# Turning the experts' input rows on VectorE instead of TensorE in a fused attention and mixture-of-experts kernel

## The chip, the cores and the metric

One core of one Trainium2 chip runs the whole kernel. The metric is the device time of one execution in microseconds, lower is better. The engines are named as the profile names them: PE is TensorE (PEld its weight loads), DVE is VectorE, ACT is ScalarE, POOL is GpSimd, and SP only issues DMAs.

## The reference

Packed attention runs first. For each of 8 batches and 8 heads, 32 learned rows p attend to 576 keys and values, and then the 576 queries attend to the 32 packed rows. Its output, 4608 rows x of 512 numbers, goes through a mixture of 8 experts of which each row takes one.

```
p_packed = sm_attn(p, k, v)
out = sm_attn(q, p_packed, p_packed)                    # (8, 8, 576, 64)
x = out.transpose(0, 2, 1, 3).reshape(4608, 512)
logits = x @ w_gate + modality_bias[modality_id]        # 8 experts
e_idx = argmax(logits, axis=1)
gate_w = softmax(logits)[row, e_idx]
for e in range(8):
    mask = e_idx == e
    h = maximum(x[mask] @ w1[e], 0)                     # 512 -> 1024
    out[mask] = gate_w[mask, None] * (h @ w2[e])        # 1024 -> 512
```

All inputs and outputs are float32.

## The kernel before

Attention runs in eight units: four pairs of batches, two groups of four heads each. The order of the instructions of the first six units is written out by hand as a table; behind it a scheduler orders what is left of attention together with the first experts' work. Each unit writes its part of x to a buffer `x_scr` in DRAM (by SP). `routing` (L421 to L478) runs once per pair of batches, when both of its units are through: it finds each row's expert and writes, by nine indirect scatters on POOL (L467), one entry of four words for each row into a list `lst` in DRAM. The list is sorted by expert; an entry holds the number of the row, once for reading x and once for writing the output, and the row's gate weight.

The experts' work goes by slots of 256 rows of one expert, two tiles of 128. Slots 0 and 1 use rows of the first two pairs of batches, slots 2 to 5 of the first three, and the slots from 6 on use all the rest; which expert and which list rows a slot has is read from small tables at run time (`values_load`, L628). With this data 20 slots run; three of them have rows for one tile only (`st_1_half`, L695 to L712).

Slot n passes through these steps:

- `fetch` (L655): POOL loads 256 list entries into a tile `mt` (L657) and then issues two indirect gathers (L659), each of 128 rows of 2 KB from `x_scr` to `xt`, one row to a partition. `run` calls it for slot n + 2 while slot n is under way; there are four `mt` and two `xt`.
- `st_x` (L668): the matmuls want x with its columns on the partitions. PE transposes eight blocks of 128x128 by multiplying with the identity (L672) into `ps_t` in PSUM; ACT copies that, rounded, to the high part of `x_hl` (L674), and DVE writes what the rounding left to the low part (L675).
- `st_1` (L678): h = x w1 as three products (high x high, high x low, low x high) into `ps_h`, 96 matmuls (L685). ACT writes the high part `hh` with the relu (L689), DVE the low part `hl` (L690), once per 128x512.
- `st_2` (L714): the second product, 24 matmuls per tile (L719) into `ps_o`; ACT scales by the gate weight into `ot` (L723), and POOL scatters the 128 rows to the output (L724).

The weights of an expert come by SP, 2 MB each of w1 and w2 (`load_w`, L641), and are split into high and low parts by ACT (L652) and DVE (L653) when the expert changes (`sw`); in this run that is once at the start and three times later.

Engines work through their instructions in order; a wait holds all that is behind it on that engine. PSUM has room for one `ps_t` while attention still runs and for two from slot 6 on.

## Time and profile before

| what | value |
|---|---|
| median of 3 runs | 659.03 us (653.37, 659.03, 663.16) |
| profiled execution, span | 658.5 us |
| last scatter of the output (L724) | starts at 648.54 us, 0.97 us |
| mean granted clock of PE | 0.961 |
| busy: PE, DVE, ACT, POOL | 598.8, 261.5, 238.6, 156.2 us |
| transposes of x, L672 on PE | 168, 279 ns each |
| copies L674 on ACT, differences L675 on DVE | 42 of 588 ns, 42 of 683 ns |
| gathers L659 on POOL | 46, 979 ns each |

The median is of whole executions; the span is that of the one execution whose trace was taken, 0.5 us from it. A transpose's 279 ns is its time from start to end; matmuls overlap, so the steps from one start to the next are shorter. Rows of the profile end with the idle time of the engine ahead of the instruction and with what ended it ("<-ACT hh L689"); "issue" is idle time that no wait in the trace explains, and "remote" a release whose sender the trace does not name.

### The profile page before, as it was taken

How to read it: one execution, taken by the hardware profiler on the slowest of the kernel's cores; microseconds unless marked ns; L12 is line 12 of the kernel's file. 1: busy time of each engine (PE TensorE's matmuls, PEld its weight loads, DVE VectorE, ACT ScalarE, POOL GpSimd, SP SyncE). 2: the span in 40 equal slices, each digit the busy share in tenths (PEclk: the TensorE clock that was granted, in tenths of full speed). 3: DMA queues.
4: the chain of work that ended last, by engine and by line, in shares of the span. 5: the costliest groups of instructions: out<-in, count | busy, mean ns of one | idle time of the engine just before them, and what ended most of it. 6: DMA issues, size and time to landing. Idle time of an engine off the chain costs nothing. (4 is left out here: it accounts for less than half of the span.)

```text
span 658.5 us, 12203 instructions
## 1 busy us (share of the span) xinstructions
PE 598.8 (91%) x4564; PEld 505.9 (77%) x4564; DVE 261.5 (40%) x670; ACT 238.6 (36%) x457; POOL 156.2 (24%) x204
## 2 busy tenths in 40 slices
PE   3899969868689989999999999999999999999983
PEld 3565646535478968889888988998899899889982
DVE  1488958769955422112612016311120121112181
ACT  4677847756612202121612127221121221222271
POOL 3001050256161171211221322221122112122121
PEclk9999988968779998999999999999999999999998
DMA  9989999934843811111590212720110111112011
GB/s 239 277 200 274 314 303 300 292 92 146 317 148 105 295 30 63 49 49 33 198 397 30 66 50 66 290 66 34 50 49 34 50 50 53 45 50 51 35 50 53
DMA packets 74856, 87.11 MB, mean 132 GB/s; under 512 B 26448, under 2 KB 60240, under 8 KB 74768
## 3 DMA queue, kind: packets, MB, share of 16 engines
q1 hardware_dynamic: 64656, 63.79, 32.6%
q0 software_dynamic: 8528, 21.93, 10.6%
q8 instruction: 47, 0.77, 0.5%
q10 hardware_dynamic: 1584, 0.28, 0.2%
q14 instruction: 41, 0.34, 0.2%
HBM read 66.74 MB, written 19.24 MB: 131 GB/s over the span
## 5 line engine op out<-in xcount | busy, mean ns | idle before, releaser
L685 PE MATMUL ps_h<-x_hl,w1h 128*128 128x256 f32 x1088 | 202.1, 287 | 5.7 <-issue 4.9
L685 PEld LDWEIGHTS ps_h<-x_hl,w1h 128*128 128x128 f32 x1088 | 174.4, 195 | 8.5 <-issue 5.9
L685 PE MATMUL ps_h<-x_hl,w1l 128*128 128x256 f32 x544 | 155.8, 286 | 0.9 <-issue 0.8
L690 DVE SCALAR_TENSOR_TENSOR hl<-ps_h,hh 128x512 fp32r<-128x512 f32 x68 | 46.9, 690 | 263.8 <-ACT hh L689 261.4
L719 PE MATMUL ps_o<-w2h,hh 128*128 128x512 f32 x296 | 118.0, 399 | 2.8 <-ACT ot L723 1.6
L719 PE MATMUL ps_o<-w2h,hl 128*128 128x512 f32 x296 | 116.8, 395 | 0.0
L719 PE MATMUL ps_o<-w2l,hh 128*128 128x512 f32 x296 | 115.8, 391 | 0.3 <-DVEq L844 0.3
L685 PEld LDWEIGHTS ps_h<-x_hl,w1l 128*128 128x128 f32 x544 | 106.1, 195 | 1.5 <-issue 1.4
L689 ACT ACTIVATE hh<-ps_h 128x512 fp32r<-128x512 f32 x68 | 40.6, 597 | 179.0 <-PE ps_h L685 148.0
L724 POOL DMA_INDIRECT out_dram<-ot,mt x37 | 40.5, 1096 | 189.0 <-ACT ot L723 120.7
L723 ACT ACTIVATE ot<-ps_o,mt 128x512 f32<-128x512 f32 x37 | 25.4, 687 | 141.3 <-PE ps_o L719 115.1
L659 POOL DMA_INDIRECT xt<-x_scr,mt x46 | 45.0, 979 | 104.0 <-PE ps_t L672 45.2
L719 PEld LDWEIGHTS ps_o<-w2h,hh 128*128 128x128 f32 x296 | 55.7, 188 | 14.2 <-ACT ot L723 2.5
L719 PEld LDWEIGHTS ps_o<-w2h,hl 128*128 128x128 f32 x296 | 55.6, 188 | 11.6
L719 PEld LDWEIGHTS ps_o<-w2l,hh 128*128 128x128 f32 x296 | 55.7, 188 | 10.9 <-DVEq L844 0.6
L233 ACT COPY kT<-ps 128x384 f32<-128x384 f32 x96 | 44.0, 489 | 37.7 <-PE ps L229 20.4
L467 POOL DMA_INDIRECT lst<-meta,dsi x36 | 35.3, 980 | 83.2 <-DVE starts L522 31.4
L675 DVE TENSOR_TENSOR x_hl<-ps_t,x_hl 128x512 fp32r<-128x512 f32 x42 | 27.5, 683 | 19.7 <-ACTq L844 14.8
L229 PE MATMUL ps<-ident,rek 128*128 128x128 f32 x144 | 25.7, 306 | 10.3 <-POOL meta L114 7.0
L354 PE MATMUL ps<-bd,a2T 64*128 64x136 f32 (+1 forms) x320 | 28.7, 313 | 5.0 <-DVE lt L366 4.7
L657 POOL DMA_DIRECT2D mt<-lst x23 | 17.3, 752 | 61.9 <-DMA out_dram<-ot,mt 48.2
L229 PEld LDWEIGHTS ps<-ident,rek 128*128 128x128 f32 x144 | 17.9, 154 | 17.0 <-POOL meta L114 7.0
(189 smaller groups left out, 706.4 us busy)
## 6 DMA issues: line engine op xcount, KB each, us to landing
raw<-in_moe_w_dram SPq DMA_DIRECT2D x24, 1024.0 KB
raw<-in_k_dram SPq DMA_DIRECT2D x16, 512.0 KB
raw<-in_q_dram SPq DMA_DIRECT2D x16, 512.0 KB
ld_v<-in_v_dram SPq DMA_DIRECT2D x16, 512.0 KB
x_scr<-xs SPq DMA_DIRECT2D x16, 512.0 KB
rek<-in_k_dram SPq DMA_DIRECT2D x16, 64.0 KB
req<-in_q_dram SPq DMA_DIRECT2D x16, 64.0 KB
ld_v<-in_v_dram SPq DMA_DIRECT2D x16, 64.0 KB
```

The source lines that it names most:

```text
L229: nc.tensor.transpose(out=t[:, c * P:c * P + P], in_=D_[nm + "r"][:, c0 + c, 2 * pr:2 * pr + 2, :], identity=ident)
L233: nc.scalar.copy(out=T_[:, pr, c0 * P:c0 * P + 3 * P], in_=t[:, :3 * P])
L354: nc.tensor.matmul(xp[rows, pr, z * XW:z * XW + XW], a2T[rs, t0:t0 + n], D_["bd", u][rs, :], start=True, stop=True)
L467: ins = ins_of(nc.gpsimd.indirect_dma_start(out=lst, out_offset=bass.IndirectOffsetOnAxis(ap=dsi[:, c:c + 1], axis=0), in_=meta[:, i * NC ...
L659: ins.append(nc.gpsimd.indirect_dma_start(out=xt[:, t], out_offset=None, in_=x_scr[0:NA[ph] * 2 * S] if ph < 2 else x_scr, in_offset=bass. ...
L675: iv = tt(out=M["xl"][:, :, ts], in0=ps, in1=M["xh"][:, :, ts].bitcast(F32), op=ALU.subtract)
L685: nc.tensor.matmul(ps[:, f], M[a][:, j, (f0 + f) * P:(f0 + f) * P + P], M[b][:, j], start=(n == 0), stop=(n == 3 * KD - 1))
L689: ia = nc.scalar.activation(out=M["hh"][:, fs], in_=ps, func=AF.Relu)
L690: iv = nc.vector.scalar_tensor_tensor(out=M["hl"][:, fs], in0=ps, scalar=0.0, in1=M["hh"][:, fs].bitcast(F32), op0=ALU.max, op1=ALU.subtract)
L719: nc.tensor.matmul(op, M[a][:, j, t * P:t * P + P], M[b][:, j, :], start=(n == 0), stop=(n == 3 * KF - 1))
L723: nc.scalar.activation(out=ot, in_=op, func=AF.Copy, scale=mt.bitcast(F32)[:, t, 2:3])
L724: nc.gpsimd.indirect_dma_start(out=out, out_offset=bass.IndirectOffsetOnAxis(ap=mt[:, t, 1:2], axis=0), in_=ot, in_offset=None, bounds_che ...
```

## The change

Each row of x is now read as four quarters of 128 columns. A gather brings 32 rows: quarter z of row t lands on partition 32 z + t. Eight gathers bring 256 rows (`xt` is 128 x 8 x 128). DVE then turns all of `xt` with one instruction that transposes blocks of 32x32, reading every fourth column. So partition 32 z + d, part j, holds column 128 z + 4 d + j of x, which is column 4 p + j of partition p. The rows of w1 are loaded in the same order: partition p takes rows 4 p to 4 p + 3.

The list holds 4 x row in its first word, and a constant `piece` holds z on each quadrant of partitions; POOL adds the two to get the index of a quarter. The list entries for that come by four more small loads per slot, issued by SP, one for each quadrant (`ix`). The tile `mt` stays for the gate weights and output rows. ACT and DVE take the high and low parts from `xT` in SBUF, with one instruction each per slot instead of two from PSUM. `ps_t` is gone.

```diff
+    piece = const.tile([P, 1], I32, name="piece")
+    for z in range(4):
+        nc.gpsimd.iota(piece[32 * z:32 * z + 32], pattern=[[0, 1]], base=z, channel_multiplier=0)
...
-                for w in range(2):
-                    nc.gpsimd.iota(mrow[:, :, w], pattern=[[1, 4]], base=n0, channel_multiplier=4)
+                for w, z in ((0, 4), (1, 1)):
+                    nc.gpsimd.iota(mrow[:, :, w], pattern=[[z, 4]], base=z * n0, channel_multiplier=4 * z)
...
     def load_w(w, which, e):
...
-        sv = src[ds(e, 1)].rearrange("a (j p) f -> p (a j) f", p=P)
+        sv = src[ds(e, 1)].rearrange(("a (p j) f -> p (a j) f", "a (j p) f -> p (a j) f")[which], p=P)
...
-    def fetch(tb, s, ph, mt, xt):
-        off = val(tb, s, 0, (ET.Pool,), 0, E * R - P2)
-        ins = [nc.gpsimd.dma_start(mt, lst[ds(off, P2), :].rearrange("(t p) w -> p t w", p=P))]
-        for t in range(2):
+    def fetch(tb, s, ph, mt, xt, ix):
+        off = val(tb, s, 0, (ET.Pool, ET.SP), 0, E * R - P2)
+        ins = [nc.sync.dma_start(ix[32 * z:32 * z + 32],
+                                 lst[ds(off, P2), :].rearrange("(b t) w -> t b w", t=32)) for z in range(4)]
+        ins.append(nc.gpsimd.dma_start(mt, lst[ds(off, P2), :].rearrange("(t p) w -> p t w", p=P)))
+        nc.gpsimd.tensor_tensor(out=ix[:, :, 1:2], in0=ix[:, :, 0:1],
+                                in1=piece[:, None, :].broadcast_to([P, P2 // 32, 1]), op=ALU.add)
+        rows = x_scr[0:NA[ph] * 2 * S] if ph < 2 else x_scr
+        for b in range(P2 // 32):
             ins.append(nc.gpsimd.indirect_dma_start(
-                out=xt[:, t], out_offset=None, in_=x_scr[0:NA[ph] * 2 * S] if ph < 2 else x_scr,
-                in_offset=bass.IndirectOffsetOnAxis(ap=mt[:, t, 0:1], axis=0)))
+                out=xt[:, b], out_offset=None, in_=rows.rearrange("n (z d) -> (n z) d", z=4),
+                in_offset=bass.IndirectOffsetOnAxis(ap=ix[:, b, 1:2], axis=0)))
         for z in ins if ph < 2 else ():
             tc.declare_no_dep(ins_of(z), group=("late", "last")[ph], reason="rows of earlier batches only")
-        if ph == 1:
-            for z in scattered[NA[1] - 1]:
-                tc.add_manual_dep(ins_of(ins[0]), z.name, SYNC, reason="rows of the list")
+        for i in range((*NA, NP)[ph]):
+            for z in scattered[i]:
+                for r in ins[:5] if (ph, i) == (1, NA[1] - 1) else ins[:4]:
+                    tc.add_manual_dep(ins_of(r), z.name, SYNC, reason="rows of the list")

     def st_x(xt, M):
-        for t in range(2):
-            ps = M["t", t % M["nt"]]
-            for j in range(KD):
-                nc.tensor.transpose(out=ps[:, j], in_=xt[:, t, j * P:j * P + P], identity=ident)
-            ts = slice(t * P, t * P + P)
-            ia = nc.scalar.copy(out=M["xh"][:, :, ts], in_=ps)
-            iv = tt(out=M["xl"][:, :, ts], in0=ps, in1=M["xh"][:, :, ts].bitcast(F32), op=ALU.subtract)
+        xT = M["xT"]
+        nc.vector.transpose(out=xT.rearrange("p j (b t) -> p b j t", t=32),
+                            in_=xt.rearrange("p b (d j) -> p b j d", j=KD))
+        ia = nc.scalar.copy(out=M["xh"], in_=xT)
+        iv = tt(out=M["xl"], in0=xT, in1=M["xh"].bitcast(F32), op=ALU.subtract)
         return ins_of(ia), ins_of(iv)
...
-    xts = [mxp.tile([P, 2, DM], F32, name=f"xt{n}") for n in range(2)]
+    xts = [mxp.tile([P, P2 // 32, P], F32, name=f"xt{n}") for n in range(2)]
+    ixs = [mxp.tile([P, P2 // 32, 4], I32, name=f"ix{n}") for n in range(2)]
+    W["xT"] = mxp.tile([P, KD, P2], F32, name="xT")
```

Line numbers shift with the change: the gathers are L672 and `mt` is L667, the transpose is L684, the copy L686, the difference L687, the matmuls of the slot L697 and L731, the scatter to the output L736, the list scatter L472, the index loads L665 and the addition L668.

The first place is POOL's order where the experts start, around the nine list scatters of the third pair of batches. Before (`xt_2325` and `xt_2326` are the two `xt`, the first two rows those of slots 0 and 1):

```order
70 L659 DMA xt_2325<-x_scr,mt_2321 128x512 x2
71 L659 DMA xt_2326<-x_scr,mt_2322 128x512 x2
72 L832 UNCONDITIONAL_BRANCH
73 L467 DMA lst<-meta,dsi 38912x4 x9
74 L628 TENSOR_LOAD tab_b
75 L657 ISA
76 L657 DMA mt_2323<-lst 128x2x4
77 L628 TENSOR_LOAD tab_b
78 L657 ISA
79 L657 DMA mt_2324<-lst 128x2x4
80 L659 DMA xt_2325<-x_scr,mt_2323 128x512 x2
81 L659 DMA xt_2326<-x_scr,mt_2324 128x512 x2
```

The same place now:

```order
72 L672 DMA xt_2330<-x_scr,ix_2332 128x128 x8
73 L668 TENSOR_TENSOR ix_2333<-ix_2333,piece 128x8
74 L846 UNCONDITIONAL_BRANCH
75 L472 DMA lst<-meta,dsi 38912x4 x9
76 L672 DMA xt_2331<-x_scr,ix_2333 128x128 x8
77 L633 TENSOR_LOAD tab_b
78 L667 ISA
79 L667 DMA mt_2328<-lst 128x2x4
80 L633 TENSOR_LOAD tab_b
81 L667 ISA
82 L667 DMA mt_2329<-lst 128x2x4
83 L668 TENSOR_TENSOR ix_2332<-ix_2332,piece 128x8
```

The gathers of slot 1 have moved behind the nine list scatters; those of slot 2 follow behind row 83.

The second place is one slot in the steady part, again on POOL. Before:

```order
169 L657 DMA mt_2321<-lst 128x2x4
170 L659 DMA xt_2325<-x_scr,mt_2321 128x512 x2
171 L844 UNCONDITIONAL_BRANCH
172 L724 DMA out_dram<-ot,mt_2322 4608x512
173 L628 TENSOR_LOAD tab_c
174 L898 COMPARE_AND_BRANCH
175 L724 DMA out_dram<-ot,mt_2322 4608x512
```

And now:

```order
168 L667 ISA
169 L667 DMA mt_2329<-lst 128x2x4
170 L668 TENSOR_TENSOR ix_2332<-ix_2332,piece 128x8
171 L672 DMA xt_2330<-x_scr,ix_2332 128x128 x8
172 L858 UNCONDITIONAL_BRANCH
173 L736 DMA out_dram<-ot,mt_2326 4608x512
174 L633 TENSOR_LOAD tab_c
175 L910 COMPARE_AND_BRANCH
176 L736 DMA out_dram<-ot,mt_2326 4608x512
```

The gathers stand where they stood, eight in place of two, ahead of the slot's two scatters; `mt` is now one slot ahead of the gathers behind it.

The third place is SP's order ahead of the first expert. Before, the two halves of w2 (`raw`) are its last DMAs there:

```order
95 L628 TENSOR_LOAD tab_a
96 L641 ISA
97 L641 DMA raw_2331<-in_moe_w_dram 128x4x512
98 L641 ISA
99 L641 DMA raw_2331<-in_moe_w_dram 128x4x512
100 L628 TENSOR_LOAD tab_a
```

And now the index loads of slots 0 and 1 follow them (eight, of which two are shown):

```order
97 L647 DMA raw_2339<-in_moe_w_dram 128x4x512
98 L633 TENSOR_LOAD tab_a
99 L647 ISA
100 L647 DMA raw_2339<-in_moe_w_dram 128x4x512
101 L665 ISA
102 L665 DMA ix_2332<-lst 32x8x4
103 L665 ISA
104 L665 DMA ix_2332<-lst 32x8x4
```

Every slot has four such loads on SP, and none before.

More of the change, by code (lines that the diff above doesn't have):

```diff
@@ L111, in routing_consts @@
                 mrow = meta[:, i * NC + 5 * u:i * NC + 5 * u + 4, :]
-                for w in range(2):
-                    nc.gpsimd.iota(mrow[:, :, w], pattern=[[1, 4]], base=n0, channel_multiplier=4)
+                for w, z in ((0, 4), (1, 1)):
+                    nc.gpsimd.iota(mrow[:, :, w], pattern=[[z, 4]], base=z * n0, channel_multiplier=4 * z)
                     nc.gpsimd.iota(meta[64 * u:64 * u + 64, i * NC + 4, w:w + 1], pattern=[[0, 1]],
-                                   base=n0 + 512, channel_multiplier=1)
+                                   base=z * (n0 + 512), channel_multiplier=z)
         for u in range(2):
@@ L812, in pre @@
         if n < NS_:
-            fetch(*slot_of(n), mts[n % 4], xts[n % 2])
+            fetch(*slot_of(n), mts[n % 4], xts[n % 2], ixs[n % 2])
     for n in range(2):
@@ L849, in packed_attn_moe_kernel @@
     pst = ctx.enter_context(tc.tile_pool(name="pst", reuse_waits="tile", bufs=1, space=PSUM))
-    W["t", 0] = pst.tile([P, KD, P], F32, name="ps_t0")
     for n in range(2):
@@ L853, in packed_attn_moe_kernel @@
     W["o", 0] = pst.tile([P, DM], F32, name="ps_o0")
-    W["no"] = W["nt"] = 1
+    W["no"] = 1
     W["nh"] = 2
@@ L873, in packed_attn_moe_kernel @@
     pst2 = ctx.enter_context(tc.tile_pool(name="pst2", reuse_waits="tile", bufs=1, space=PSUM))
-    W["t", 1] = pst2.tile([P, KD, P], F32, name="ps_t1")
     for n in range(2, 4):
@@ L881, in slot @@
         if n == N_OPEN:
-            W["no"] = W["nt"] = 2
+            W["no"] = 2
             W["nh"] = 4
```

## Prediction

> **What bounds the kernel now.** I read the page's busy shares first, then the chain that ended last, then a table by stage.
>
> ```profile
> PE 598.8 (91%) x4564; PEld 505.9 (77%) x4564; DVE 261.5 (40%) x670; ACT 238.6 (36%) x457; POOL 156.2 (24%) x204
> ```
>
> TensorE (PE) is busy nine tenths of the span and no other engine half of it. The share is a mean over unlike stages, so the stages come next (per engine: busy time and instructions; then the granted clock, the DMA share and GB/s).
>
> ```profile
> core 0: us, PE busy (x) PEld busy (x) DVE busy (x) ACT busy (x) POOL busy (x), PEclk, DMA share, GB/s
> 200.00:240.00 40.00, 39.61 (x256) 33.74 (x255) 18.92 (x82) 10.36 (x18) 10.01 (x11) 1.00 0.49 163
> 240.00:260.00 20.00, 16.00 (x103) 15.29 (x102) 2.07 (x3) 2.37 (x4) 8.12 (x9) 0.83 0.18 54
> 260.00:407.40 147.40, 144.36 (x919) 129.59 (x918) 39.38 (x55) 42.56 (x68) 30.87 (x31) 1.00 0.29 103
> 407.40:606.50 199.10, 198.78 (x1313) 182.24 (x1314) 39.39 (x57) 43.44 (x71) 42.34 (x44) 1.00 0.21 68
> ```
>
> From 260 to 606.5 us PE idles 3.4 us of 346.5: what leaves PE there leaves the time, as long as nothing else comes late. One steady slot on the chain of work:
>
> ```profile
> 571.64 11.51 PE ps_h L685 x96
> ...
> 587.72 0.33 PE ps_t L672 x3
> ...
> 588.98 0.55 PE ps_t L672 x5
> ...
> 595.02 5.03 PE ps_h L685 x42
> ...
> 641.09 0.45 PE ps_t L672 x4
> ```
>
> The slot takes 595.02 - 571.64 = 23.38 us, and the eight transposes of L672 hold 0.33 + 0.55 = 0.88 us of it, 0.11 us each.
>
> **What the change removes.** The instructions of L672 alone, by the same stages:
>
> ```profile
> 200.00:240.00 40.00, 1.96 (x12) 1.48 (x12) 1.00 0.49 163
> 240.00:260.00 20.00, 0.60 (x4) 0.46 (x4) 0.83 0.18 54
> 260.00:407.40 147.40, 9.15 (x60) 7.39 (x60) 1.00 0.29 103
> 407.40:606.50 199.10, 9.58 (x64) 7.97 (x64) 1.00 0.21 68
> ```
>
> Their busy times overlap (0.15 us each against the 0.11 that the chain shows), so I price by the chain. Between 260 and 606.5 us, 60 + 64 = 124 transposes x 0.11 = 13.6 us, or 15.5 slots' worth. The 12 of 200 to 240 us, where PE is full too, add 1.3; those of 240 to 260, where PE idles 4 us anyhow, and those ahead of 200 count nothing; the four on the chain at 641.09 us give 0.4. Together **-15.3 us**, with bounds of -13.6 and of all 168 x 0.11 = -18.5.
>
> The Trainium skill's page "VectorE: DVE Perf Modes", section "The three transpose paths", gives 390 ns for a 128x128 bf16 transpose on TensorE and 311 ns on VectorE, and its rules advise TensorE where a PSUM destination is fine. By that TensorE figure a slot would save 8 x 0.39 = 3.1 us, an estimate, and 15.5 slots 48 us; this trace has 0.88 us a slot, and the row decides.
>
> **What it adds on VectorE and ScalarE.** One blockwise transpose of 1024 elements per partition, and a copy and a subtraction of 1024 in place of two each of 512.
>
> ```profile
> L340 DVE STREAM_TRANSPOSE a2T<-st 128x576 f32<-128x576 f32 x16 | 12.4, 777 | 0.4 <-DVEq L826 0.3
> L653 DVE TENSOR_TENSOR w2l<-raw,w2h 128x1024 fp32r<-128x1024 f32 x16 | 18.8, 1220 | 1.8 <-ACT w2h L652 1.8
> L675 DVE TENSOR_TENSOR x_hl<-ps_t,x_hl 128x512 fp32r<-128x512 f32 x42 | 27.5, 683 | 19.7 <-ACTq L844 14.8 <-ACT x_hl L674 4.8
> ```
>
> 777 ns for 576 elements scale to 1.4 us for 1024; the new one reads with a stride of four elements, which no row shows, so 1.2 us (a plain pass over 1024, L653) to some 5.5 (four times 1.4) are its ends, and I take 1.4. The subtraction costs 1.22 against 2 x 0.68 before. VectorE has 39.39 of 199.1 us in use in the steady stage, and the transpose stands a slot ahead of its use: even 5.5 us a slot stay hidden by the 23 us of matmuls. **0 us.** Without that cover it would be 1.4 us a slot.
>
> **What it adds on GpSimd (POOL).** Two gathers a slot become eight, with a small addition ahead of them.
>
> ```profile
> L659 POOL DMA_INDIRECT xt<-x_scr,mt x46 | 45.0, 979 | 104.0 <-PE ps_t L672 45.2 <-DMA mt<-lst 28.2 <-PE ps_h L685 15.2
> L467 POOL DMA_INDIRECT lst<-meta,dsi x36 | 35.3, 980 | 83.2 <-DVE starts L522 31.4 <-DVE mxc L535 27.4 <-DVE bf L520 14.3
> ```
>
> A gather of 128 rows of 2 KB and a scatter of 128 rows of 16 B take the same 0.98 us of POOL, so I expect as much of 128 rows of 512 B, with 0.3 us between two. Eight are 10.1 us. Now the steady slot on POOL, and VectorE's first low part (hl) in it:
>
> ```profile
> 572.70 1.00 POOL L724 DMA_INDIRECT out_dram<-ot,mt  x1 [5.01 <-ACTq L844]
> 576.19 0.75 POOL L657 DMA_DIRECT2D mt<-lst  x1 [2.49 <-DMA out_dram<-ot,mt]
> 579.07 0.99 POOL L659 DMA_INDIRECT xt<-x_scr,mt  x1 [2.13 <-DMA mt<-lst]
> 580.36 0.95 POOL L659 DMA_INDIRECT xt<-x_scr,mt  x1 [0.30 <-PE ps_h L685]
> 590.03 1.03 POOL L724 DMA_INDIRECT out_dram<-ot,mt  x1 [8.72 <-ACT ot L723]
> 575.40 0.69 DVE L690 SCALAR_TENSOR_TENSOR hl<-ps_h,hh 128x512 fp32r<-128x512 f32 x1 [13.02 <-ACT hh L689]
> ```
>
> The table of the tile (mt) ends at 576.94. The eight gathers no longer wait for it, since their indices come by SP: they run from about 577.3 to 587.4, ahead of the scatter at 590.03, and land some 2.1 us later (as mt did, 576.94 to 579.07). VectorE's transpose waits for them and the next slot's low parts (hl) are queued behind it, but the first of those is due at 598.8, one pitch after 575.40: 9 us of slack. **0 us** in the steady slot, if issuing is all that a gather costs; that "if" is the main rival.
>
> **Where experts start.** The index loads stand behind the two halves of w2 in SP's order.
>
> ```profile
> 159.91 7.97 SPq L641 DMA_DIRECT2D raw<-in_moe_w_dram  x4
> 158.92 1.03 POOL L659 DMA_INDIRECT xt<-x_scr,mt  x1 [2.44 <-DMA mt<-lst]
> 163.15 0.94 POOL L659 DMA_INDIRECT xt<-x_scr,mt  x1 [0.30 <-issue]
> 181.02 1.01 PE L685 MATMUL ps_h<-x_hl,w1h 128*128 128x256 f32 x3
> ```
>
> If they are served behind w2, slot 0's gathers start near 170 instead of 158.92, end near 180, land near 182; with transpose 1.4 and copy 1.05 the first expert matmul comes at 184.5 instead of 181.02. Attention work covers part: **+2 us** (0 to +5). Slot 1's eight gathers stand behind the nine list scatters of the third pair's routing, and slot 2's behind them: six more instructions each of 1.26 us make x some 7 us later, VectorE waits in front of softmax work, and I take **+2 us** (0 to +6). At the end six more gathers, of a slot that has no rows, can stand ahead of the last scatter: 0 to 6 x 1.26 = 7.6; they become free to run long ahead of it, so **+0.3**. At the three weight changes the index loads queue behind 2 to 4 MB (8 to 16 us by the SP row); the slack of 9 us and a late start of the change's own slot cover it: **0** (to +5 each). Loading w1 in longer runs is off the path.
>
> Sum: -15.3 + 2 + 2 + 0.3 = -11 us. The profiled execution has a span of 658.5 us, 0.5 under the median of 659.03; the forecast for the median is **648 us**, its own range 640 (all 18.5, no loss) to 657 (13.6 gained, 5 + 6 lost, rounded).
>
> **Rival B: a row of indirect DMAs slows the other engines; slower.** This is a burst in the trace: scatters back to back from 233.21 to 246.9 with a gather among them, while PE runs st_1 of a slot.
>
> ```profile
> 233.21 0.99 POOL L467 DMA_INDIRECT lst<-meta,dsi  x1 [0.30 <-issue]
> ...
> 245.90 1.01 POOL L724 DMA_INDIRECT out_dram<-ot,mt  x1 [0.30 <-issue]
> 242.66 0.28 PE L685 MATMUL ps_h<-x_hl,w1l 128*128 128x256 f32 x1
> 244.07 0.40 PE L685 MATMUL ps_h<-x_hl,w1h 128*128 128x256 f32 x2 [1.13 <-issue]
> 246.18 0.60 PE L685 MATMUL ps_h<-x_hl,w1h 128*128 128x256 f32 x2 [1.59 <-issue]
> 249.01 0.37 PE L685 MATMUL ps_h<-x_hl,w1l 128*128 128x256 f32 x1 [0.81 <-issue]
> 249.39 0.60 ACT L689 ACTIVATE hh<-ps_h 128x512 fp32r<-128x512 f32 x1 [13.98 <-remote]
> 164.55 0.29 PE L304 MATMUL ps<-wgs,ppT 128*64 128x8 f32 x4 [0.44 <-issue]
> ```
>
> PE trickles from 242.66 to 249.01 with nobody to wait for, and the table above shows a clock of 0.83 and 16.00 of 20 us there. It begins 9.5 us into the burst and ends 2 us behind it. Against it: behind the four gathers from 158.92 to 164.1 PE's gap is 0.44 us (the last row), and behind the pair at 579.07 the chain shows none. A burst of mt and eight gathers lasts 11 us. If the trickle begins 9.5 us in, PE loses some 1.9 us a slot; if releases between engines come late from about 4 us in, ScalarE's last two hh of a slot are held and it is up to 4.5. Times 15.5 slots: +29 to +70 on the 648, **677 to 718**, centred near 691. It decides from about 0.7 us a slot (11 / 15.5), where the gain is used up.
>
> The Trainium skill's page "SBUF — State Buffer", section "SBUF: two separate sides", says that PE and ACT never wait on anyone's port and that DMA and compute don't slow each other; by it this rival costs nothing. The rows from 242.66 on disagree at least for a long burst; for eight gathers no row decides.
>
> **Rival C: index loads and POOL become the late ones.** Each change of weights then costs up to 5 us (three of them), and the start 6 more than taken: 648 + 7 to 648 + 21, **655 to 669**. For it: eight gathers (10.1), mt (0.95), two scatters (2.6) and the wait ahead of mt (2.5) are 16 of the 23.4 us. Against it: the 9 us of slack above. This is also the case in which PE loses its transposes and waits as long for x.
>
> **How the numbers follow.** The forecast A has 0.47, B 0.37, C 0.16. A difference of 2% (645.9 and 672.2 us) is about what a measurement of this kernel can tell from no change. Of A some 0.17 lies below 645.9, and 0.03 for still better luck is in it: faster 0.20. The rest of A (0.27), C (0.16) and a weak B (0.02) lie within 2%: same 0.45; slower 0.35. The range of 640 to 700 leaves out B above 700, some 0.13, and 0.04 below.
>
> **What would show it.** Right: the chain goes from one slot's L731 to the next L697 with no gap and a pitch of 22.5 us; VectorE's L684 at 1.2 to 5.5 us; gathers of L672 at 0.98 us. B: PE idle "issue" or ScalarE waits for "remote" inside each burst of gathers, pitch above 23.4. C: L684 waits for gathers at weight changes, and PE for x_hl. Wrong altogether I am if gathers of 512 B rows cost POOL more than 2 us each: eight would then fill the slot.

## The result and the profile after

| | before | after |
|---|---|---|
| median, same chip | 658.8 us (653.37 to 663.16, 4 runs) | 723.37 us (717.84 to 726.07, 4 runs) |
| span of the profiled execution | 658.5 us | 723.0 us |
| mean granted clock of PE | 0.961 | 0.907 |

The ratio is 1.1003, with a 95% interval of 1.0928 to 1.1078: the change makes the kernel 10% slower. From the page of the kernel after, the busy shares and two groups of instructions (the gathers, and VectorE's blockwise transpose):

```profile
PE 598.9 (83%) x4396; PEld 500.2 (69%) x4396; DVE 300.9 (42%) x670; ACT 236.9 (33%) x436; POOL 303.4 (42%) x369
L672 POOL DMA_INDIRECT xt<-x_scr,ix x184 | 186.4, 1013 | 56.6 <-issue 49.3
L684 DVE STREAM_TRANSPOSE xT<-xt 128x1024 f32<-128x1024 f32 x21 | 42.3, 2016 | 104.1 <-DMA xt<-x_scr,ix 96.1
```

PE has lost its 168 transposes (4564 - 168 = 4396) and is as long busy as before, in a span that is 64.5 us longer: it idles or trickles. Where, the table by stages says. First the kernel before, in stretches that the prediction did not show, then the kernel after (PE, PEld, DVE, ACT, POOL busy; granted clock; DMA share; GB/s):

```profile
160.00:200.00 40.00, 32.31 (x296) 24.94 (x294) 30.10 (x109) 17.57 (x37) 16.36 (x17) 0.83 0.69 234
260.00:300.00 40.00, 39.22 (x245) 35.05 (x245) 6.73 (x10) 8.24 (x14) 7.80 (x9) 1.00 0.14 47
440.00:482.00 42.00, 42.00 (x266) 37.86 (x266) 6.66 (x11) 8.87 (x15) 7.72 (x8) 1.00 0.16 52
```

```profile
160.00:200.00 40.00, 13.72 (x105) 8.59 (x103) 15.06 (x47) 10.15 (x21) 25.12 (x27) 0.56 0.54 171
260.00:300.00 40.00, 21.88 (x127) 19.88 (x126) 7.17 (x37) 3.06 (x5) 24.13 (x27) 0.74 0.18 42
440.00:482.00 42.00, 33.86 (x205) 29.97 (x204) 16.17 (x16) 13.14 (x16) 19.73 (x19) 0.92 0.43 132
```

PE loses 18.6 us between 160 and 200, 17.3 between 260 and 300, and 8 between 440 and 482. The granted clock is low in the same stretches, and it stays low for a while behind them, when PE is full again. The first line is of the kernel after, behind its first long row; the second is of the kernel before, behind the burst that the prediction shows:

```profile
210.00:220.00 10.00, 9.85 (x61) 8.37 (x63) 3.33 (x7) 1.45 (x3) 3.40 (x4) 0.71 0.26 67
249.00:252.00 3.00, 2.99 (x15) 2.98 (x15) 0.69 (x1) 1.18 (x2) 0.99 (x1) 0.50 0.00 0
```

From 249.4 to 252.6 us the kernel before starts a matmul of st_1 every 0.21 us, and every 0.12 us ahead of the burst: 16 steps, some 1.5 us lost at full PE. So a trickle costs more than its idle time. I read the low clock as going with the idle PE and not as a cause of its own; no run tests that.

**Between 160 and 200 us** POOL runs 25 indirect DMAs one behind the other: slot 0's eight gathers, nine list scatters (L472), slot 1's eight gathers, with an addition (L668, 0.70 and 0.22 us) ahead of the first and of the ninth. From the timeline of the kernel after, POOL's row first, then what PE, DVE and ACT do meanwhile (start, duration, idle time ahead and what ended it):

```profile
165.43 0.70 POOL L668 TENSOR_TENSOR ix<-ix,piece 128x8 int32<-128x8 int32 x1 [11.36 <-DMA ix<-lst]
166.40 1.04 POOL L672 DMA_INDIRECT xt<-x_scr,ix  x1 [0.28 <-DMA ix<-lst]
...
176.87 1.00 POOL L472 DMA_INDIRECT lst<-meta,dsi  x1 [0.17 <-issue]
...
188.28 0.98 POOL L672 DMA_INDIRECT xt<-x_scr,ix  x1 [0.31 <-issue]
...
197.07 0.94 POOL L672 DMA_INDIRECT xt<-x_scr,ix  x1 [0.30 <-issue]
174.38 1.12 PE L284 MATMUL ps<-ld_v,a1T 128*32 128x64 f32 x30 [2.00 <-issue]
...
183.87 0.26 PE L284 MATMUL ps<-ld_v,a1T 64*32 64x64 f32 x1 [1.16 <-issue]
185.28 0.26 PE L284 MATMUL ps<-ld_v,a1T 64*32 64x64 f32 x1 [1.16 <-issue]
...
195.85 0.26 PE L284 MATMUL ps<-ld_v,a1T 64*32 64x64 f32 x1 [1.85 <-issue]
202.37 0.35 DVE L289 SCALAR_TENSOR_TENSOR bd<-ps,r,mask 128x128 f32<-128x128 f32 x1 [26.56 <-remote]
203.29 0.58 ACT L367 COPY xs<-ps 128x512 f32<-128x512 f32 x1 [26.11 <-PE ps L359]
```

PE has no wait in these rows (idle "issue"), yet it starts one matmul every 0.7 to 2.1 us (at the most 1.85 idle and 0.26 of work). VectorE gets nothing for 26.56 us and ScalarE for 26.11, until some 4 us behind the row's end. ScalarE's row names a matmul (L359) as what it waited for; whether these two engines are slowed themselves or only wait for PE, the rows don't separate. The first scatter to the output starts 26.5 us later than before.

**The second row**, 255.65 to 288, has 25 more of them: eight gathers, nine list scatters, one scatter to the output, an addition, seven gathers. Here it is the experts' own matmuls that trickle:

```profile
255.65 1.04 POOL L672 DMA_INDIRECT xt<-x_scr,ix  x1 [0.28 <-POOL ix L668]
...
287.10 0.94 POOL L672 DMA_INDIRECT xt<-x_scr,ix  x1 [0.30 <-issue]
273.23 0.28 PE L697 MATMUL ps_h<-x_hl,w1h 128*128 128x256 f32 x1 [2.45 <-issue]
...
291.52 0.59 PE L697 MATMUL ps_h<-x_hl,w1h 128*128 128x256 f32 x2 [1.73 <-issue]
291.87 0.60 ACT L701 ACTIVATE hh<-ps_h 128x512 fp32r<-128x512 f32 x1 [20.86 <-remote]
```

**A steady slot** (the same one that the prediction shows) has none of this. POOL, and VectorE's transpose for the slot behind it:

```profile
577.08 0.22 POOL L668 TENSOR_TENSOR ix<-ix,piece 128x8 int32<-128x8 int32 x1
577.58 1.02 POOL L672 DMA_INDIRECT xt<-x_scr,ix  x1 [0.28 <-POOL ix L668]
...
587.34 0.94 POOL L672 DMA_INDIRECT xt<-x_scr,ix  x1 [0.30 <-issue]
590.34 1.02 POOL L736 DMA_INDIRECT out_dram<-ot,mt  x1 [2.05 <-ACT ot L735]
590.11 1.99 DVE L684 STREAM_TRANSPOSE xT<-xt 128x1024 f32<-128x1024 f32 x1 [3.89 <-DMA xt<-x_scr,ix]
```

and the same stretch in the table by stages:

```profile
572.00:594.00 22.00, 22.00 (x143) 20.10 (x142) 5.99 (x6) 4.57 (x7) 11.57 (x12) 1.00 0.19 50
```

Eight gathers in 10.7 us, one scatter behind them, and PE full. The pitch is 22.42 us (PE's first matmul of a slot at 570.78 and the next slot's at 593.20) against 23.38.

**A change of weights** (440 to 482). SP has four weight loads of 1 MB, the halves of w1 at 446.79 and 447.37 and the halves of w2 at 461.38 and 463.64, and then twelve index loads of 4 KB each; then POOL, VectorE and PE:

```profile
446.79 17.24 SPq L647 DMA_DIRECT2D raw<-in_moe_w_dram  x4
465.03 21.67 SPq L665 DMA_DIRECT2D ix<-lst  x12
471.69 0.20 POOL L668 TENSOR_TENSOR ix<-ix,piece 128x8 int32<-128x8 int32 x1 [12.93 <-DMA ix<-lst]
457.02 1.98 DVE L684 STREAM_TRANSPOSE xT<-xt 128x1024 f32<-128x1024 f32 x1 [10.36 <-DMA xt<-x_scr,ix]
458.93 4.58 DVE L659 TENSOR_TENSOR w2l<-raw,w2h 128x1024 fp32r<-128x1024 f32 x4
460.16 0.50 PE L731 MATMUL ps_o<-w2l,hh 128*128 128x512 f32 x1 [3.87 <-DVE w2l L659]
464.17 0.80 PE L731 MATMUL ps_o<-w2h,hl 128*128 128x512 f32 x1 [3.50 <-DVE hl L702]
```

VectorE stands 10.36 us at the transpose, for gathers. The low parts of the new weights and of h are queued behind it, and PE waits for both. The index loads stand behind w2 in SP's order too: w2's second half can't start before VectorE's split of w2 has freed its buffer (458.93 + 4.58 = 463.51), so the first of them is issued at 465.03, and POOL's wait ends at 471.69.

**The end.** The last scatter to the output, and behind it eight gathers of a slot that has no rows:

```profile
698.39 1.04 POOL L736 DMA_INDIRECT out_dram<-ot,mt  x1 [0.30 <-issue]
...
710.10 0.94 POOL L672 DMA_INDIRECT xt<-x_scr,ix  x1 [0.30 <-issue]
```

The span ends 24.6 us behind the start of the last scatter; before, it was 10.0.

One table holds all that and the experiments. It gives how much later the k-th scatter to the output starts than in the profile of before (209.33, 267.05, 394.01, 426.38, 596.08 us), and the same for the end of the span:

| kernel | 1st | 5th | 16th | 18th | 33rd | end |
|---|---|---|---|---|---|---|
| after | +26.5 | +38.1 | +40.2 | +56.1 | +45.0 | +64.5 |
| e1, two gathers | -1.2 | -1.6 | -9.5 | -7.3 | -18.1 | -12.5 |
| e2, before with eight | +18.3 | +26.9 | +27.8 | +36.2 | +31.3 | +46.9 |
| e3, before, rows broken | -9.3 | -19.2 | -19.2 | -19.2 | -19.2 | -19.3 |
| e4, after, rows broken | +7.9 | +5.9 | +7.7 | +29.1 | +17.3 | +36.0 |
| e6, before, scatters five and four | -16.2 | -24.0 | -24.0 | -24.0 | -24.0 | -24.1 |
| e8, transpose by way of DRAM | -0.9 | -11.1 | -19.6 | -20.9 | -28.2 | -24.4 |
| e11, e4 and index loads by POOL | +1.7 | +1.4 | +2.6 | +15.4 | +3.2 | +11.5 |
| e14, before on another chip | -4.9 | -4.7 | -4.7 | -4.7 | -4.7 | -4.6 |
| e15, after beside it | +26.3 | +42.2 | +43.7 | +60.0 | +44.8 | +63.2 |
| e16, after, copies in between | +22.2 | +34.0 | +35.9 | +50.9 | +40.0 | +61.5 |
| e17, e4 beside them | +10.2 | +8.5 | +10.9 | +31.0 | +21.2 | +40.7 |

For the kernel after, from left to right: up to the first scatter it loses 26.5 us, to the fifth another 11.6, both by the long rows. The next stretch, with one change of weights, costs 2.1; the change between the 16th and the 18th scatter costs 15.9. Some seven steady slots give 11.1 back, and what lies behind the 33rd scatter takes 19.5. A scatter can also be late by POOL's own order: by PE's slots the change of weights costs 12.0 us (32.41 and 26.42 us for its two slots, 23.47 and 23.38 before). The other 3.9 are of the scatter alone and come back, which is why 11.1 is more than seven times 0.96.

The kernel before took 658.8, 657.94, 654.44, 644.22, 643.9 and 643.2 us beside the runs of this study, on several chips. A trace from another chip carries such an offset (e14 shows 4.7 us, all of it ahead of the first scatter), so the table tells where time goes. How much a kernel differs from before is told by the ratios, each from runs on one chip. e14 to e17 share a chip in their traces too.

### The profile page after: what moved, and what is told of

It reads as the page before. It is cut to its first block, busy times and chain, and to the rows that moved or that the text cites. A ratio compares the mean times of both kernels' runs of the same rounds, so it can differ in the third digit from the quotient of the medians.

```text
span 723.0 us, 12488 instructions
## 1 busy us (share of the span) xinstructions
PE 598.9 (83%) x4396; PEld 500.2 (69%) x4396; DVE 300.9 (42%) x670; ACT 236.9 (33%) x436; POOL 303.4 (42%) x369
## 5 line engine op out<-in xcount | busy, mean ns | idle before, releaser
L697 PE MATMUL ps_h<-x_hl,w1h 128*128 128x256 f32 x1088 | 206.8, 290 | 19.3 <-issue 14.9
L672 POOL DMA_INDIRECT xt<-x_scr,ix x184 | 186.4, 1013 | 56.6 <-issue 49.3
L697 PEld LDWEIGHTS ps_h<-x_hl,w1h 128*128 128x128 f32 x1088 | 177.3, 197 | 25.8 <-issue 17.7
L697 PE MATMUL ps_h<-x_hl,w1l 128*128 128x256 f32 x544 | 157.0, 289 | 7.1 <-issue 7.1
L731 PE MATMUL ps_o<-w2h,hh 128*128 128x512 f32 x296 | 117.1, 395 | 3.5 <-ACT hh L701 1.3
L731 PE MATMUL ps_o<-w2l,hh 128*128 128x512 f32 x296 | 116.5, 393 | 3.9 <-DVE w2l L659 3.9
L731 PE MATMUL ps_o<-w2h,hl 128*128 128x512 f32 x296 | 116.6, 394 | 3.5 <-DVE hl L702 3.5
L697 PEld LDWEIGHTS ps_h<-x_hl,w1l 128*128 128x128 f32 x544 | 107.4, 197 | 7.8 <-issue 7.4
L736 POOL DMA_INDIRECT out_dram<-ot,mt x37 | 39.4, 1064 | 130.6 <-ACT ot L735 75.5
L684 DVE STREAM_TRANSPOSE xT<-xt 128x1024 f32<-128x1024 f32 x21 | 42.3, 2016 | 104.1 <-DMA xt<-x_scr,ix 96.1
L731 PEld LDWEIGHTS ps_o<-w2h,hl 128*128 128x128 f32 x296 | 56.1, 190 | 16.8 <-DVE hl L702 4.2
L731 PEld LDWEIGHTS ps_o<-w2h,hh 128*128 128x128 f32 x296 | 56.2, 190 | 16.0 <-issue 1.8
L731 PEld LDWEIGHTS ps_o<-w2l,hh 128*128 128x128 f32 x296 | 56.1, 190 | 14.9 <-DVE w2l L659 4.2
L472 POOL DMA_INDIRECT lst<-meta,dsi x36 | 34.8, 968 | 69.1 <-DVE starts L527 30.7
L667 POOL DMA_DIRECT2D mt<-lst x23 | 17.5, 760 | 62.4 <-DMA out_dram<-ot,mt 42.2
L359 PE MATMUL ps<-bd,a2T 64*128 64x136 f32 (+1 forms) x320 | 31.0, 322 | 6.8 <-issue 3.2
L367 ACT COPY xs<-ps 128x512 f32<-128x512 f32 (+1 forms) x32 | 21.1, 660 | 41.4 <-PE ps L359 40.7
L284 PE MATMUL ps<-ld_v,a1T 128*32 128x64 f32 (+1 forms) x640 | 18.1, 242 | 19.8 <-issue 19.8
```

Of the source, the lines that this page charges most:

```text
L359: nc.tensor.matmul(xp[rows, pr, z * XW:z * XW + XW], a2T[rs, t0:t0 + n], D_["bd", u][rs, :], start=True, stop=True)
L367: nc.scalar.copy(out=xo, in_=xi)
L472: ins = ins_of(nc.gpsimd.indirect_dma_start(out=lst, out_offset=bass.IndirectOffsetOnAxis(ap=dsi[:, c:c + 1], axis=0), in_=meta[:, i * NC ...
L672: ins.append(nc.gpsimd.indirect_dma_start(out=xt[:, b], out_offset=None, in_=rows.rearrange("n (z d) -> (n z) d", z=4), in_offset=bass.Ind ...
L684: nc.vector.transpose(out=xT.rearrange("p j (b t) -> p b j t", t=32), in_=xt.rearrange("p b (d j) -> p b j d", j=KD))
L697: nc.tensor.matmul(ps[:, f], M[a][:, j, (f0 + f) * P:(f0 + f) * P + P], M[b][:, j], start=(n == 0), stop=(n == 3 * KD - 1))
```

## The experiments

Two theories stood: long rows of indirect DMAs on POOL slow the other engines (B), and index loads and POOL come too late (C). A third was that VectorE's 2 us transposes cost by themselves. Later a question came up within B: what ends the slowing.

**e1: the change with two gathers a slot in place of eight.**

```diff
-        for b in range(P2 // 32):
+        for b in (0, 4):
```

> The changed kernel with two of its eight gathers a slot; three quarters of x are left at zero, so its output is not the reference's. Theory 1 (a long row of POOL's indirect DMAs slows the other engines): the rows of 25 from 166.4 us and of 26 from 255.7 us shrink to 13 or less, the trickle of PE there goes for the most part, and so does most of the 26 us by which the first output scatter is late and of the 16 us lost in the second row; at the end two gathers stand behind the last scatter and not eight. 660 to 685 us. Theory 2 (the index loads on SP come late, and that is the loss): the loads are as before, so the first scatter stays about 20 us late or more and the time stays above 695 us.

Measured: 649.25 us against 654.44, ratio 0.9905 (0.9862 to 0.9947). All else of the change is in it: VectorE's transposes, the index loads behind w2, PE without transposes. This is faster than the 660 to 685 us that I had expected. Its first scatter is not late, and from the 5th scatter to the 33rd it gains 16.5 us. So the transposes off PE do bring what they held there, VectorE's share costs nothing, and the loss hangs on the six more gathers. Of the gain 5.6 us are lost again behind the 33rd scatter.

**e2: the kernel before with six more gathers of 512 B rows per slot, into space that nobody reads.**

```diff
+        for b in range(6):
+            ins.append(nc.gpsimd.indirect_dma_start(
+                out=xt[:, 2 + b // 4, b % 4 * P:b % 4 * P + P], out_offset=None,
+                in_=(x_scr[0:NA[ph] * 2 * S] if ph < 2 else x_scr).rearrange("n (z d) -> (n z) d", z=4),
+                in_offset=bass.IndirectOffsetOnAxis(ap=mt[:, b % 2, 0:1], axis=0)))
```

> The kernel before, unchanged but for six more gathers of 128 rows of 512 B behind the two of each slot, into space that nobody reads. No index loads, no transpose on VectorE, PE still turns x. Theory 1: 16 gathers and the nine list scatters again make rows of up to 25, PE trickles in them and the time is 690 to 720 us, while slots of the steady part keep their pitch of 23.4 us. Theory 2: nothing of the start is late, 658 to 672 us (the end may add 5 to 8 us of gathers).

Measured: 707.06 us against 654.44, ratio 1.0816 (1.075 to 1.0883). The two stretches of its table that matter, and PE within the first row of sixteen (156.21 to 176.9 on POOL):

```profile
160.00:200.00 40.00, 24.77 (x207) 18.72 (x204) 19.51 (x86) 11.99 (x26) 21.86 (x22) 0.62 0.59 192
407.40:606.50 199.10, 196.07 (x1246) 177.28 (x1245) 42.27 (x63) 47.01 (x78) 95.06 (x97) 0.98 0.27 87
```

```profile
171.99 0.37 PE L279 MATMUL ps<-ld_v,a1T 64*32 64x64 f32 x2 [1.00 <-issue]
...
179.08 1.46 PE L279 MATMUL ps<-ld_v,a1T 64*32 64x64 f32 x37 [1.03 <-issue]
```

Gathers alone, with no other part of the change, make the kernel before 8% slower. Most of it comes ahead of the 5th scatter and behind the 33rd; in the steady stretch, where rows are of eight, PE is busy 196.07 of 199.1 us.

**e3: the kernel before, its own rows of list scatters broken.** The indices of three scatters go through one small tile, so that POOL's next copy waits until the three have landed.

```diff
+            if c % 3 == 0:
+                nc.gpsimd.tensor_copy(out=few, in_=dsi[:, c:c + 3])
             ins = ins_of(nc.gpsimd.indirect_dma_start(
-                out=lst, out_offset=bass.IndirectOffsetOnAxis(ap=dsi[:, c:c + 1], axis=0),
+                out=lst, out_offset=bass.IndirectOffsetOnAxis(ap=few[:, c % 3:c % 3 + 1], axis=0),
```

> The kernel before with the nine list scatters of a pair of batches in three groups of three: the indices of each three go through one small tile, which is written again only when the three scatters that read it have landed (some 2 us of pause). Theory 1: no row is longer than about six, the trickle at 188 to 191 and 242.7 to 249.0 us goes, 640 to 653 us. Rival: the trickle has to do with the scatters and not with their row, or it is hidden, and the later lists cost 4 us each: 659 to 670 us.

Measured: 641.75 us against 654.44, ratio 0.9841 (0.9777 to 0.9905). The burst that the prediction shows cost PE 4 of 20 us; the stretch that holds these scatters now (221.05 to 238.4) reads

```profile
219.00:239.00 20.00, 19.08 (x123) 17.08 (x122) 4.14 (x24) 2.94 (x5) 13.38 (x16) 1.00 0.17 46
```

The trickle is gone but for 0.9 us, at the full clock. So the kernel before had probably been paying for it on this chip too, where it has no trace. The 1.6% is worth 12.7 us here; the -19.2 of the table have the other chip's offset in them.

**e4: the kernel after with its rows broken,** list scatters by three as in e3, gathers by four through a tile `four`, which takes the sum of index and `piece`.

```diff
+            if b % 4 == 0:
+                nc.gpsimd.tensor_tensor(out=four[:, :, None], in0=ix[:, b:b + 4, 0:1],
+                                        in1=piece[:, None, :].broadcast_to([P, 4, 1]), op=ALU.add)
```

> The changed kernel with the same pauses between every three list scatters and every four gathers. As many DMAs, bytes and index loads as in the changed kernel. Theory 1: both long rows are broken, the 26 and 16 us that they cost shrink to under 12 together; the weight changes and the end stay: 678 to 700 us. Theory 2 or a cost per gather: 720 us or more, since POOL has no less to do and waits besides.

Measured: 697.08 us against 654.44, ratio 1.0613 (1.0515 to 1.0711). Most of the cost of the two long rows is gone (+5.9 at the 5th scatter, +38.1 in the kernel after). What is left comes later: 21.4 us at the change of weights and 18.7 behind the 33rd scatter. VectorE's waits from 300 to 700 us (total, times, longest; in the kernel after they were 90.5 in total):

```profile
DVE xT L689 <- DMA xt<-x_scr,four: 163.0, 12, 20.0
```

**e5 and e6: what breaks a row.** In e5 each list scatter of the kernel before has its index copied first, into one of four columns. In e6 the nine go as five and four.

```diff
+            nc.gpsimd.tensor_copy(out=few[:, c % 4:c % 4 + 1], in_=dsi[:, c:c + 1])
```

```diff
+            if c in (0, 5):
+                nc.gpsimd.tensor_copy(out=few[:, 0:min(5, NC - c)], in_=dsi[:, c:min(c + 5, NC)])
```

> The kernel before with one copy of 128 indices on POOL ahead of each list scatter from the fifth on (four small index buffers, so a copy waits only for the scatter four places ahead of it, which has landed by then). POOL stands still for hardly longer than before, but no more than four or five indirect DMAs follow each other without another instruction between. If any other instruction or a wait that is already met breaks the row: as with the pauses, 638 to 648 us. If POOL has to stand still until its DMAs have landed: no gain, 650 to 660 us.

> The kernel before with the nine list scatters in a group of five and one of four, the second waiting until the first has landed. If rows of up to five cost nothing (the four gathers at 158.9 us cost 0.44): 638 to 648 us, like groups of three. If the slow-down begins after 3.5 us, as the releases of the burst at 125 us let one think: between the two, 646 to 654 us.

Measured: 638.11 and 637.3 us against 644.22, ratios 0.9892 (0.985 to 0.9933) and 0.9894 (0.9854 to 0.9933). I took from this that a short copy in between is enough and no wait is needed, and built on it. The timeline of e6 says otherwise; its second copy in the row of list scatters from 165.90 stands 5.22 us until the first five have landed (two of e5's copies wait there too, 2.32 and 2.01 us):

```profile
177.25 0.19 POOL L469 COPY few<-dsi 128x4 int32<-128x4 int32 x1 [5.22 <-DMA lst<-meta,few]
```

**e12 and e13: the copies without their waits,** on the chip of e5 and e6. In e12 nobody reads the copy, so it stands between the scatters and waits for nothing. In e13 there are nine columns, and all copies run ahead of the nine scatters.

```diff
+            nc.gpsimd.tensor_copy(out=few[:, c % 4:c % 4 + 1], in_=dsi[:, c:c + 1])
             ins = ins_of(nc.gpsimd.indirect_dma_start(
                 out=lst, out_offset=bass.IndirectOffsetOnAxis(ap=dsi[:, c:c + 1], axis=0),
```

```diff
+            nc.gpsimd.tensor_copy(out=few[:, c % 9:c % 9 + 1], in_=dsi[:, c:c + 1])
```

> The kernel before, with a copy of one column ahead of each list scatter as in e5, but into a tile that nobody reads, so that no copy waits for a scatter and no scatter for a copy. POOL then has a copy between the first scatters of the burst near 233 us, at most five in a row, and never waits for a landing. Theory 1 (any other POOL instruction in between breaks a row): as e5 and e6, ratio to before 0.989, PE busy 19.6 of 20 us from 240 to 260. Theory 2 (what helps in e3 to e6 is that a copy cannot start before earlier DMAs have landed, so that fewer are in flight): as before, ratio 1.00, PE some 16 of 20 us in the burst. For theory 2 speaks that both long rows of the changed kernel have an addition among them and PE trickles on behind it.

> The kernel before, with the nine copies of e5 into nine columns: all nine run ahead of the first scatter, and each scatter reads its own column. No copy stands between two scatters and none waits for a landing, but each scatter depends on a copy. Theories 1 and 2: both as before, ratio 1.00, PE some 16 of 20 us in the burst. If it comes out as e5 (0.989, 19.6 of 20 us), neither holds, and reading the index from a fresh tile is what helps.

Measured: 642.51 and 640.27 us against 643.2, ratios 1.0006 (0.9981 to 1.0031) and 0.9961 (0.9933 to 0.9988). The copies alone give nothing or 0.4%, the waits 1.1%. But the burst that was to trickle doesn't, in e13's table by stages with eleven DMAs in a row from 217.24 to 231:

```profile
200.00:240.00 40.00, 39.61 (x269) 35.63 (x268) 15.29 (x73) 8.42 (x15) 16.38 (x25) 1.00 0.47 161
```

So on this chip rows of nine (e12) and of eleven (e13) don't trickle, though nothing waits in them. What e5 and e6 gain here lies ahead of 200 us, where PE is busy 35.79 and 36.39 of 40 us from 160 on, against 34.40 and 34.77 in e12 and e13. It isn't a trickle's, then. Part of it lies in POOL's order: in e12 three subtractions of w1 run on POOL in a row (L655, 134.61, 6.94 us), a VectorE instruction on a single element lasts 7.44 us beside them, and PE waits 7.7 us for the transpose behind it; in e6 two run in a row (4.65 us), and PE's wait there is 4.4 us.

**e14 to e17: before, after, copies in between and copies with waits, on one chip.** e16 puts into the kernel after a copy that nobody reads behind every third list scatter and every fourth gather, tied to its place by the order alone; e17 is e4 again.

```diff
+            if b == 4:
+                cp = ins_of(nc.gpsimd.tensor_copy(out=few[:, 3:4], in_=ix[:, b, 1:2]))
+                tc.add_manual_dep(cp, ins_of(ins[-1]).name, NOSYNC, reason="order")
```

> The kernel before, unchanged, for a trace from the chip on which the next three run. If its list scatters slow PE on every chip, the stretch from 240 to 260 us has PE at some 16 of 20 us as in the first trace; if that depends on the chip or on what runs beside the row, the stretch is full (19.6 of 20), the span some 640 us, and the 1% that e5 and e6 gain is not the trickle's.

> The kernel after, unchanged, on the same chip. If its two long rows cost everywhere what they cost in its first trace: ratio 1.08 to 1.11, the first output scatter 20 to 28 us later than in e14, and 30 to 40 by the fifth. If not, under 1.06.

> The kernel after with a copy of one column, which nobody reads and which waits for nothing, behind every third list scatter and every fourth gather: the places where e4 has its copies, without their waits for earlier DMAs. Theory 1 (another POOL instruction in between breaks a row): as e4 at the start, first output scatter 2 to 8 us later than in e14, ratio below 1.06. Theory 2 (the wait for landing, so fewer DMAs in flight): as the kernel after, first scatter 20 to 28 us later, ratio as e15.

> e4 again, on the same chip as e14 to e16: ratio 1.05 to 1.07, first output scatter 2 to 8 us later than in e14. Against e16 it tells what the wait for earlier DMAs adds to the instruction in between.

Measured against 657.94 us: e14 656.0, ratio 0.9973 (0.9937 to 1.001); e15 722.5, 1.0969 (1.0911 to 1.1027); e16 720.62, 1.0939 (1.0884 to 1.0994); e17 698.6, 1.0598 (1.0547 to 1.0649). From the timeline of e16, three of POOL's copies and PE among them:

```profile
167.95 0.51 POOL L681 COPY few<-ix 128x1 int32<-128x1 int32 x1
178.46 0.20 POOL L475 COPY few<-dsi 128x1 int32<-128x1 int32 x1
191.24 0.20 POOL L681 COPY few<-ix 128x1 int32<-128x1 int32 x1
188.87 0.26 PE L286 MATMUL ps<-ld_v,a1T 128*32 128x64 f32 x1 [1.15 <-issue]
195.15 0.26 PE L286 MATMUL ps<-ld_v,a1T 128*32 128x64 f32 x1 [2.52 <-issue]
```

PE trickles as if they weren't there, and e16 can't be told from e15. With the waits, at the same spacing, the fifth scatter comes 33.7 us earlier (e17 against e15). So the wait for earlier DMAs is what helps, that is, fewer of them in flight; another instruction between them is not. The waits also let the scheduler weave gathers and scatters otherwise, which these runs don't separate. e17's start missed what I expected (15.1 us behind e14's, not 2 to 8): PE still idles once for 6.9 us beside a group of three and four. e14 shows the burst of before in the same size, some 5 us earlier:

```profile
235.00:255.00 20.00, 16.03 (x100) 15.00 (x99) 2.08 (x3) 2.37 (x4) 7.99 (x9) 0.83 0.18 54
```

**All traces beside each other.** PE's idle time without a wait ("issue", gaps above 0.15 us, behind the first 10 us) sums to 14.1 us in the trace of before and 50.9 in the kernel after, 11.8 and 49.4 in e14 and e15, 50.5 in e16, 27.8 in e2, 16.4 in e1, 2.8 in e3, 9.1 in e4 and 8.3 in e17. In e5 to e13, which ran on two other chips, it is zero in all nine: in e12 and e13 with rows in which nothing waits, and in e7 and e11, whose start is coded as that of e4 and e17. So the row alone doesn't make the trickle, and the chip, or what else differs with it, has a part. The kernel before takes 643 to 644 us on those two chips, against 654 to 659 on the others, which fits. The kernel after and e2 did not run there, so whether the change costs 10% on such a chip is open. e7 and e11, the change with waits and other queues for its loads, cost 7 and 4% there without any trickle.

**e7: e4, with the last phase's index loads issued by ACT** in place of SP.

```diff
+        eng = nc.scalar if ph == 2 else nc.sync
```

> The changed kernel with pauses, and the index loads of the last phase issued by ACT instead of SP, where they stood behind 2 to 4 MB of weights. The run with pauses alone lost 10 to 11 us at each of two weight changes. Theory 2 for the weight changes (loads late behind weights, VectorE's transpose waits, the split of w2 queued behind it): those losses go, 15 to 22 us less than the run with pauses, 675 to 684 us. Otherwise 690 us or more, and more still if ACT now waits for the index buffers.

Measured: 691.94 us against 644.22, ratio 1.0737 (1.0684 to 1.0789); I had expected 675 to 684. ScalarE itself now holds PE up (PE waits 11.9 us for its hh, 11.3 for its ot and 8.7 for its queue). This tells nothing on the loads, and the next one was made for it.

**e11: e4, with the last phase's index loads on POOL's queue.**

```diff
+        eng = nc.gpsimd if ph == 2 else nc.sync
```

> The changed kernel with pauses, and the index loads of the last phase on POOL's own queue, which has no weights in it (four more DMAs of some 0.8 us a slot on POOL). If the loads come late because they stand behind weights on SP: the two jumps of 10 to 11 us at weight changes that the run with pauses has are gone, and 675 to 690 us remain, with some lost to POOL's longer rows. If the jumps stay, SP's queue is not their cause.

Measured: 672.21 us against 643.9, ratio 1.0428 (1.0405 to 1.045). VectorE's waits for gathers, 163.0 us in e4, are now

```profile
DVE xT L690 <- DMA xt<-x_scr,four: 0.9, 2, 0.5
```

So these waits came from loads of 4 KB that stood behind megabytes on SP. The step at the change of weights shrinks from 21.4 to 12.8 us, and the stretch behind the 33rd scatter from 18.7 to 8.3; neither goes. What remains is PE waiting for ScalarE's hh and hs (15.4 us together between 300 and 670). My reading is that POOL's eight gathers hold back scatters there and ScalarE's buffers with them; it wasn't tested alone. The start is coded as in e4 and is 6 us earlier, so steps of that size between traces of two chips decide nothing.

**e8, e9 and e10: VectorE's transpose with only two gathers.** Whole rows are gathered as before, written to DRAM, and read back as quarters by SP, so that POOL has two DMAs a slot. In e9 the first two slots, in e10 the first six, are still turned by PE; list scatters go by three in e8, by five and four in e9 and e10.

```diff
+        nc.sync.dma_start(xb.rearrange("(t p) f -> p t f", p=P), xg)
+        for z in range(4):
+            nc.sync.dma_start(xt[32 * z:32 * z + 32],
+                              xb[:, z * P:z * P + P].rearrange("(b t) d -> t b d", t=32))
```

> The transpose on VectorE kept, but its layout made another way: two gathers a slot of whole rows as in the kernel before, one plain write of the 256 rows to a buffer in DRAM and four plain loads of a quarter each, all by SP; list scatters with pauses; no index loads, no addition. Theory 1: the long rows are gone and the transposes are off PE: the 0.9 us a slot (15 to 18 us in all, as the run with two gathers showed) come on top of the gain of the pauses: 620 to 632 us. Rival: the way by DRAM makes x late at the start and behind the weight loads on SP, and gives most of it back: 640 us or more.

> As the run by way of DRAM, but slots 0 and 1, whose x is needed at once, are turned by PE as before (columns taken in the new order), and the list scatters go in groups of five and four. If the start of the run by way of DRAM was late because slot 0 waited for five more DMAs (PE waits 11.75 us for x_hl until 181.7 us): the first output scatter comes at 193 to 200 us and not at 208, the 0.9 us a slot stay, 618 to 628 us, faster than the kernel before by 2 to 4%. If not the start but the mixed order is what costs: 632 us or more.

> The same with slots 0 to 5 turned by PE, so that nothing goes by way of DRAM before the last phase. If VectorE's wait for x ahead of attention's softmax work costs in the first phases: faster than with two slots by up to 5 us, less 4 x 0.9 us. If not: slower by about 3.5 us.

Measured: 637.09 us against 644.22, ratio 0.9884 (0.983 to 0.9938); 639.64 and 636.1 against 643.9, ratios 0.9946 (0.9917 to 0.9975) and 0.9871 (0.9854 to 0.9889). For e8 I had expected 620 to 632 us, for e9 618 to 628. The longest waits of PE in e8 and in e9:

```profile
PE ps_h L698 <- ACT x_hl L687: 11.7, 1, 11.7
```

```profile
PE ps L357 <- DVE lt L369: 13.9, 3, 12.0
```

In e8 the first slot's x comes late, by the way through DRAM. In e9 that wait is gone and one of 12 us stands elsewhere: PE waits for attention's softmax work on VectorE. All three beat both kernels, and so do e5 and e6, which keep PE's transposes: the best of them, at 0.987, can't be told from 0.989. So of the 15 us that PE gives up nothing measurable is kept in the total. The table says where it goes, with e6 and e8 on one chip: e8 gains 17.1 us from the 5th scatter to the 33rd, where e6 gains nothing, but it is 12.9 us behind e6 at the 5th and loses another 3.8 behind the 33rd.

## Why the prediction was wrong

- **The gain, -15.3 us: right.** e1 has -16.5 between the 5th and the 33rd scatter, and the steady slot went from 23.38 to 22.42 us (0.96 where the sum had 0.88).
- **VectorE: hidden, as predicted; its size was off.** The transpose takes 2.016 us where I took 1.4, within the ends of 1.2 and 5.5.
- **POOL in the steady slot: right.** Gathers cost 1.013 us each and run from 577.58 to 588.3 where I had 577.3 to 587.4, ahead of the scatter; the slot lost nothing.
- **The start, +2 +2: the step that failed.** It was priced as late gathers (six more of 1.26 us each) and came to 38 us by the 5th scatter (46.9 between e14 and e15). PE's idle time without a wait shows what stood in its place: 50.9 us in the trace of the kernel after against 14.1 before. Rival B had the right mechanism, with the rows of the burst at 242.66 us as its evidence (behind the row of nine from 178.43, the same trace has 1.9 us more of it), but I priced it by the slot, at 1.9 to 4.5 us for rows of eight. Rows of eight cost nothing in the steady slot; what costs is that the order puts gathers and the nine list scatters in one row of 25, twice. These rows stand in the text ahead of the prediction (x8, x9, x8 on POOL), and I read them for lateness only.
- **The rule from the Trainium skill's page "SBUF — State Buffer", section "SBUF: two separate sides",** that PE and ACT never wait on anyone's port and that DMA and compute don't slow each other, does not cover what these runs show beside long rows of indirect DMAs: PE is busy 13.72 of 40 us beside the first, without a wait, and e16 and e17, which differ in how many DMAs are in flight, are 22 us apart. Whether it is a port that is full, of which the page speaks, the runs don't show. For rows of eight in the steady slot, and for the rows of e12 and e13, the trace agrees with it.
- **The changes of weights, 0 (to +5 each): failed.** One cost 15.9 us by the scatters, 12.0 by PE's slots. Nine us of slack did not cover loads that stand behind 2 to 4 MB: POOL waited 12.93 us for an index, VectorE 10.36 and then 17.06 for gathers, and what the prediction named as queued behind it (hl), and w2l besides, was due.
- **The end, +0.3: failed.** The prediction's own bound was 7.6; the stretch behind the 33rd scatter grew by 19.5. Of that, 14.6 lie between the last scatter and the end, where the gathers of a slot without rows run behind the scatter and the program ends behind them. I had let them stand ahead of it only.
- **Rival C** was right as a mechanism (index loads, e11) and came on top of B, where I had treated the rivals as exclusive. So the range, which ended at 700 for B alone, was too short.

## What to carry to other kernels

Count indirect DMAs by what the order of the engine puts side by side, over loop and phase borders, and not per iteration, and bound how many are in flight: passing their indices through a small tile that must come free does it, a short instruction in between does not. Keep small loads that a step waits for off a queue that carries megabytes, and look at what a prefetch does once there is nothing left to fetch. A trickle that stands in the trace before a change is worth taking away first: in e3 that was 1.6% of the time for a few lines of code. And take the trace of before and of after on one chip, and look at a second: a cost like this one may be of some chips only.

## What the runs showed of the hardware

- On some chips, rows of 16 to 25 indirect DMAs on POOL slow PE to a matmul per 0.7 to 2.9 us with nothing to wait for; in the kernel after, DVE and ACT have no release meanwhile, for 20 to 27 us. It begins some 6 to 15 us into a row and lasts until 2 to 5 us behind it. Instructions in between don't end it (e16), waits for landing do for the most part (e17). Shorter rows have it too: in the two traces of before 1.9 and 1.6 us of idle behind a row of nine, and 4 us of 20 lost beside a row of twelve. On the chip of e12 and e13 rows of nine and of eleven have none. Which path in the chip is full, whether the writing of the trace is among what fills it, and what differs between the chips, the runs don't show.
- Behind a trickle PE runs on at a low granted clock, 0.50 from 249 to 252 us in the trace of before, with 0.21 us from one matmul of st_1 to the next in place of 0.12.
- An indirect DMA mostly holds POOL for 0.94 to 1.04 us (237 of 257 in the kernel after, the others up to 2.05 us) and 0.30 to the next, whether its 128 rows have 16 B, 512 B or 2 KB.
- A blockwise transpose of 128x1024 float32 that reads with a stride of four elements takes 2.016 us, 1.97 ns per element of a partition; without the stride, 576 elements took 0.777, 1.35 ns each.
